# A mixture-of-experts block loop: lists, row split, scaling, gather and transposes in another order

## The chip, the cores and the metric

The kernel runs on one core of a Trainium2 chip. The core has five engines with a queue each: TensorE (PE) multiplies matrices into PSUM, VectorE (DVE) and ScalarE (ACT) work element by element, GpSimd (POOL) does small operations and issues gathers and scatters by index, SyncE (SP) issues the other DMAs. Each engine takes its instructions strictly in program order and waits on semaphores of the others. The metric is the device time of one execution in microseconds; the median of several runs counts.

## What is computed

An attention over pooled keys and values gives rows x of 512 numbers, one a token (8 x 576 = 4608 tokens). Each token is sent to one of 8 experts: a gate picks one, or the token keeps its predecessor's. The part that the change touches is what comes then, for each token:

```python
h = np.maximum(x[b, s] @ w1[e], 0.0)     # 512 -> 1024
out[b, s] = p[e] * (h @ w2[e])           # 1024 -> 512, scaled by the gate's weight
```

Inputs and outputs are float32. The products run on numbers split in two (a high and a low part, the three larger of the four products kept).

## The kernel before

The first 200 us or so are the attention and the routing; they write the rows x to memory (`x_rows`) and the tokens of each expert to lists (`ids`). Then come blocks of 256 listed rows of one expert, in two halves of 128, or of 128 rows alone at the end of an expert's list. Three blocks run in code ahead of the loop; the loop `For_i` runs the others, 14 with two halves and 5 with one in this execution. All instructions of the loop stand in the order in which they are written (`manual_schedule`), for each engine.

Names: `W1` and `W2` are the weights split into high and low tiles (`w1h`, `w1l`, `w2h`, `w2l` in rows), `raw1` and `raw2` the next expert's weights as they arrive (`raw`), `xt` (`x` in rows) the rows split and turned, `ht` the hidden values split (`ht_h`, `ht_l`), `hp` the PSUM tiles of layer 1 (six of them), `o_ps` the two PSUM tiles of layer 2, `ob` the scaled output, `m_a`, `m_b`, `m_c`, `m_d` the lists (token number and weight) of four blocks that follow each other, `idp` a list as it arrives, `idk` row numbers for the gather, `xg` gathered rows, `xd` their copy in memory, `xq` the copy read back in pieces of 32 columns, `xs` the pieces transposed.

A pass of the loop for block j, before the change:

- `entry(iv, 0)` loads from a table whether the block has one or two halves; TensorE, ScalarE and VectorE branch by it.
- `head(j)`: VectorE takes the list that was fetched in the block before (`ids_take`, L295, `row_numbers`, L292); SyncE fetches the list of block j + 3 (`lists`, L289); GpSimd touches `xg` (`seen_x`, L1084), writes into it (`fetch`, L1098 and L1099) and gathers rows (L299).
- Two halves (`two_halves`): eight times eight matmuls of layer 1 (L322, L324), each followed by ScalarE and VectorE (`l1_h`, `l1_l`, L329 to L335), the transposes of `xq` by quarters in between (`squares`, L310), then layer 2 of the second half (`l2(1)`, L346). One half (`l1_one`): 24 matmuls of layer 1 (L976), ReLU (L981), VectorE's transpose of the whole `xq` (L982), eight transposes on TensorE (L985), the split into `ht` (L990, L991).
- `rest(j)`: SyncE writes the gathered rows to `xd` and reads them back in pieces (`rows_pieces`, L303, `pieces_rows`, L307). `changes` loads whether the next block has another expert. If so, `weights1` splits W1 (ScalarE casts, L172, VectorE subtracts, L173) and SyncE fetches further weights (L165). VectorE shifts the lists (`meta_shift`, L1093 to L1095, and L1165), scales the second half's output (`emit_scale(1)`, L1078), and GpSimd scatters it (`emit_rows`, L1087 to L1089). `next_rows` splits the next block's rows (L315, L316). TensorE does layer 2 of the first half (`l2(0)`), `weights2` splits W2 (L177, L178) and SyncE fetches (L169), then follow `emit_scale(0)` and `emit_rows(0)`.

So each queue holds a block's work in this order; a waiting instruction holds up all that stands behind it on its engine. SyncE doesn't wait for TensorE itself and runs ahead into the next block until a gather or a list that isn't taken stops it.

## Time and profile before

| | us |
|---|---|
| median of 3 runs (624.92 to 626.41) | 625.03 |
| profiled execution | 623.03 |
| its span | 621.3 |
| TensorE busy in it | 594.5 |
| VectorE busy | 439.7 |
| ScalarE busy | 291.8 |
| GpSimd busy | 273.6 |

The span is the time from the first instruction to the last; the execution's own time lies around it. Busy times of different engines overlap. A row of a timeline gives the start, the length, the engine, the line in the code, the operation with what it writes and reads, and in brackets how long the engine stood idle before it and what ended that. A matmul's end is modelled, so its length overlaps the next one.

### The profile page before, as it was taken

To read this page: it belongs to the slowest core of one execution; us is meant where nothing else is said; L and a number is where in the kernel's file an instruction comes from. 1 tells how busy PE (TensorE), PEld (TensorE's weight loads), DVE (VectorE), ACT (ScalarE), POOL (GpSimd) and SP (SyncE) were. 2 spreads that over 40 slices of the span, in tenths; PEclk is the share of its full clock that TensorE was granted. 3 is DMA by queue.
4 is the path that set the end of the run, shared out by engine and by line. 5 is a ranking of instruction groups with operands and counts; after the bars stand their busy time and mean duration, and the time that the engine had idled before them with its cause. 6 is when DMAs were issued, how large, how long until landed. Compare 5 with 4: busy or idle time off the path is not lost. (4 is left out here: it accounts for less than half of the span.)

```text
span 621.3 us, 14355 instructions
## 1 busy us (share of the span) xinstructions
PE 594.5 (96%) x3386; PEld 509.3 (82%) x3387; DVE 439.7 (71%) x1035; ACT 291.8 (47%) x697; POOL 273.6 (44%) x505
## 2 busy tenths in 40 slices
PE   8999999999999999999999999999999999999991
PEld 7898988898878878888887877787888888888870
DVE  7899898999766426565885686889556686654781
ACT  2777777965433313242742373746233363422550
POOL 6686776776673425134134326132352213341242
PEclk9999999999999999999999999999999999999996
DMA  8998973975003584331663486577543385322403
GB/s 340 356 383 303 365 276 103 318 173 204 19 2 102 176 301 135 102 118 68 211 228 113 143 259 219 186 242 267 196 127 105 101 258 195 115 71 85 118 27 99
DMA packets 62009, 111.95 MB, mean 180 GB/s; under 512 B 13466, under 2 KB 33946, under 8 KB 61980
## 3 DMA queue, kind: packets, MB, share of 16 engines
q1 hardware_dynamic: 53468, 89.54, 43.5%
q0 software_dynamic: 8512, 22.07, 11.0%
q8 instruction: 13, 0.21, 0.1%
q14 instruction: 16, 0.13, 0.1%
HBM read 81.88 MB, written 31.80 MB: 183 GB/s over the span
## 5 line engine op out<-in xcount | busy, mean ns | idle before, releaser
L322 PE MATMUL hp<-x,w1h 128*128 128x512 f32 x364 | 130.7, 400 | 2.5 <-DVE x L316 2.5
L346 PE MATMUL o_ps<-w2h,ht_h 128*128 128x512 f32 x312 | 122.8, 393 | 1.2 <-ACT ht_h L990 1.2
L346 PE MATMUL o_ps<-w2l,ht_h 128*128 128x512 f32 x312 | 122.1, 391 | 0.4 <-DVE w2l L178 0.2
L324 PE MATMUL hp<-x,w1l 128*128 128x256 f32 x364 | 102.2, 281 | 0.0
L329 ACT COPY hs<-hp 128x256 f32<-128x256 f32 x91 | 33.4, 369 | 125.8 <-PE hp L324 120.5
L346 PE MATMUL o_ps<-w2h,ht_l 128*128 128x512 f32 x312 | 87.8, 391 | 1.4 <-DVE ht_l L991 1.4
L322 PEld LDWEIGHTS hp<-x,w1h 128*128 128x128 f32 x364 | 68.4, 188 | 20.4 <-issue 3.8
L334 ACT ACTIVATE ht_h<-hs 128x256 fp32r<-128x256 f32 x136 | 57.1, 420 | 37.5 <-DVE hs L330 30.4
L1087 POOL TENSOR_TENSOR m_e<-m_i,zi 128x1 int32<-128x1 int32 x42 | 8.5, 201 | 142.3 <-DVE m_i L292 136.4
L346 PEld LDWEIGHTS o_ps<-w2h,ht_h 128*128 128x128 f32 x312 | 58.6, 188 | 14.6 <-issue 2.2
L346 PEld LDWEIGHTS o_ps<-w2h,ht_l 128*128 128x128 f32 x312 | 58.4, 188 | 14.5 <-DVE ht_l L991 2.2
L1078 DVE TENSOR_SCALAR ob<-o_ps,m_a 128x512 f32<-128x512 f32 x42 | 31.5, 750 | 53.9 <-PE o_ps L346 50.6
L324 PEld LDWEIGHTS hp<-x,w1l 128*128 128x128 f32 x364 | 68.9, 189 | 0.7
L346 PEld LDWEIGHTS o_ps<-w2l,ht_h 128*128 128x128 f32 x312 | 58.7, 188 | 12.5 <-DVE w2l L178 1.3
L565 PE MATMUL op<-vaug,aT 128*128 128x148 f32 (+4 forms) x448 | 66.0, 306 | 0.7 <-ACT osb L367 0.6
L565 PEld LDWEIGHTS op<-vaug,aT 128*128 128x128 f32 (+1 forms) x448 | 60.0, 179 | 3.9 <-issue 1.3
L335 DVE SCALAR_TENSOR_TENSOR ht_l<-hs,ht_h 128x256 fp32r<-128x256 f32 x136 | 56.4, 416 | 5.9 <-ACT ht_h L334 5.5
L1088 POOL TENSOR_TENSOR zf<-m_e,ob 128x1 f32<-128x1 f32 x42 | 13.9, 331 | 96.1 <-DVE ob L1078 65.2
L1089 POOL DMA_INDIRECT out<-ob,m_e x42 | 45.8, 1091 | 18.8 <-issue 18.8
L330 DVE TENSOR_TENSOR hs<-hp,hs 128x256 f32<-128x256 f32 x91 | 37.3, 417 | 19.9 <-ACT hs L329 11.5
L704 POOL DMA_INDIRECT ids<-pm,pos x36 | 38.7, 1076 | 17.0 <-DVE pos L699 8.0
L299 POOL DMA_INDIRECT vt_in<-x_rows,idk x40 | 39.8, 995 | 10.1 <-issue 8.1
(256 smaller groups left out, 1170.2 us busy)
## 6 DMA issues: line engine op xcount, KB each, us to landing
raw<-in_moe_w SPq DMA_DIRECT2D x48, 512.0 KB
xd<-vt_in SPq DMA_DIRECT2D x20, 512.0 KB
vt_in<-xd SPq DMA_DIRECT2D x80, 128.0 KB
kk<-in_k SPq DMA_DIRECT2D x16, 576.0 KB
qt<-in_q SPq DMA_DIRECT2D x16, 512.0 KB
vt_in<-in_v SPq DMA_DIRECT2D x16, 512.0 KB
x_rows<-xs SPq DMA_DIRECT2D x16, 512.0 KB
vt_in<-in_v_st SPq DMA_DIRECT2D x8, 256.0 KB
```

What stands on the lines that cost most here:

```text
L299: nc.gpsimd.indirect_dma_start(out=xg[:, h, :], out_offset=None, in_=x_rows[0:NT + 1], in_offset=bass.IndirectOffsetOnAxis(ap=idk[:, h:h + ...
L322: nc.tensor.matmul(out=ps, lhsT=W1[0][:, kk, f * P:(f + 1) * P], rhs=xt[:, kk].rearrange("p i n -> p (i n)"), start=(kk == 0), stop=False, ...
L324: nc.tensor.matmul(out=ps[:, 0:2 * P], lhsT=W1[1][:, kk, f * P:(f + 1) * P], rhs=xt[:, kk, 0, :], start=False, stop=(kk == KD - 1), skip_g ...
L329: nc.scalar.copy(out=hb[:, 0, :], in_=ps[:, 2 * P:])
L330: nc.vector.tensor_tensor(out=hb[:, 1, :], in0=ps[:, 0:2 * P], in1=hb[:, 0, :], op=ALU.add)
L334: nc.scalar.activation(out=ht[0][:, f, :], in_=hb, func=AF.Relu)
L335: nc.vector.scalar_tensor_tensor(out=ht[1][:, f, :], in0=hb, scalar=0.0, in1=ht[0][:, f, :].bitcast(F32), op0=ALU.max, op1=ALU.subtract)
L346: nc.tensor.matmul(out=to[h], lhsT=ht[i][:, kk, h * P:(h + 1) * P], rhs=W2[j][:, kk, :], start=(n == 0), stop=(n == 3 * KF - 1))
L565: nc.tensor.matmul(out=out, lhsT=lhs, rhs=rhs if len(out.shape) == 3 else rhs.rearrange("p s x -> p (s x)"), start=all(x[0] != n for x in ...
L704: ins = nc.gpsimd.indirect_dma_start(out=ids.rearrange("t m w -> (t m) w"), out_offset=bass.IndirectOffsetOnAxis(ap=pos[:, u:u + 1], axis= ...
L1078: nc.vector.tensor_scalar(out=ob[:, h, :], in0=o_ps[h], scalar1=m_a[:, h, 1:2], scalar2=None, op0=ALU.mult)
L1089: return nc.gpsimd.indirect_dma_start(out=outv, out_offset=bass.IndirectOffsetOnAxis(ap=m_e[h][:, 0:1], axis=0), in_=ob[:, h, :], in_offse ...
```

## The change

Nothing is computed otherwise. The list fetched for block j + 3 is taken in block j's `rest`, ahead of the splits of new weights (`take`), and the shift of the lists goes there too; `changes` is loaded at the block's head. SyncE writes `xd` at the head, for rows gathered in the block before. `next_rows` comes ahead of `emit_scale(1)`. Layer 2 of the first half is cut in two: hidden columns 0 to 3 go into the two branches, 4 to 7 stay in `rest`, and behind them GpSimd touches `xg` and gathers (`seen_x`, `fetch`). ScalarE does `emit_scale(0)`. In `l1_one` VectorE's transpose of `xq` comes first, the first four TensorE transposes stand in the middle of layer 1's second half, the other four in the middle of the first part of layer 2, and ReLU runs on 512 columns at once. The block ahead of the loop follows the same `rest`.

```diff
-    def l2(h, kks=range(KF), to=None):
+    def l2(h, kks=range(KF), to=None, part=None):
...
         n = 3 * kks[0]
+        if part:
+            jobs = [jobs[x] for x in part]
+            n += part[0]
...
         def l1_one():
-            for f in range(2):
...
-                for c in range(1 + f):
-                    w = 512 // (1 + f)
-                    nc.scalar.activation(out=hs[:, f * 512 + c * w:f * 512 + (c + 1) * w], in_=hp[f][:, c * w:(c + 1) * w], func=AF.Relu)
-            nc.vector.transpose(out=xs, in_=xq.rearrange("p m (j k) -> p k m j", k=KD))
...
-            turn(0, hp[2])
-            turn(1, hp[5])
...
+            nc.vector.transpose(out=xs, in_=xq.rearrange("p m (j k) -> p k m j", k=KD))
...
+            layer1(0, range(12))
+            relu(0)
+            layer1(1, range(6))
+            turn(0)
+            layer1(1, range(6, 12))
+            relu(1)
+            l2(0, range(4), part=range(6))
+            turn(1)
+            l2(0, range(4), part=range(6, 12))
...
-        def emit_scale(h):
+        def emit_scale(h, late=False):
+            if late:
+                nc.scalar.activation(out=ob[:, h, :], in_=o_ps[h], func=AF.Copy, scale=m_a[:, h, 1:2])
+                return
...
-    def head(j, seen=True):
-        if seen:
-            seen_x(0)
-            seen_x(1)
+    def take():
         ids_take(m_d)
         row_numbers(idk, m_d)
-        lists(j + 3)
-        fetch()
-
-    def rest(j, turned=False):
-        rows_pieces()
+
+    def rest(j, change, begin=False):
+        if begin:
+            rows_pieces()
         pieces_rows()
-        chg, nx = changes(j)
-        first(chg, nx)
         meta_shift()
         nc.vector.tensor_copy(out=m_c, in_=m_d)
-        if turned:
+        take()
+        first(*change)
+        if begin:
             for c2 in range(2):
                 rows_split(c2, hp[3 + c2], xt)
+        else:
+            next_rows()
         seen_o(0)
         emit_scale(1)
         first_half = emit_rows(1)
-        if not turned:
-            next_rows()
-        l2(0)
+        l2(0, range(4, KF))
+        for h in range(2):
+            seen_x(h)
+        fetch()
+        chg, nx = change
         with tc.If(chg > 0):
             weights2(chg, nx)
-        emit_scale(0)
+        emit_scale(0, late=True)
...
             if begin and f == 3:
-                head(1, False)
+                take()
+                lists(4)
+                fetch()
...
         l2(1)
+        if begin:
+            for c2 in range(2):
+                rows_turn(c2, xgs["f"], hp[3 + c2])
+        l2(0, range(4))
...
-            head(iv)
+            change = changes(iv)
+            lists(iv + 3)
+            rows_pieces()
```

On VectorE, in `rest` of a loop block: the shift of the lists, the scaling and the split of the rows, behind W1's splits (rows of REGISTER_ALU and ISA are the queue's own bookkeeping; numbers behind a name tell tiles apart). Before:

```order
L1147 UNCONDITIONAL_BRANCH
L1093 COPY m_a<-m_b 128x4
L292 REGISTER_ALU
L292 CAST m_i<-m_b 128x2
L1095 REGISTER_ALU
L1095 COPY m_b<-m_c 128x4
L1165 REGISTER_ALU
L1165 COPY m_c<-m_d 128x4
L1078 REGISTER_ALU
L1078 TENSOR_SCALAR ob<-o_ps_2348,m_a 128x512
L316 REGISTER_ALU
L316 TENSOR_TENSOR x_2506<-vt_in,x_2506 128x2x256
```

And in the change, from the last shift on:

```order
L1175 COPY m_c<-m_d 128x4
L295 REGISTER_ALU
L295 COPY m_d<-idp 128x4
L292 REGISTER_ALU
L292 CAST idk<-m_d 128x2
L1163 COMPARE_AND_BRANCH
L173 REGISTER_ALU
L173 TENSOR_TENSOR w1l<-raw_2936,w1h 128x1024
...
L316 TENSOR_TENSOR x_2506<-vt_in,x_2506 128x2x256
L1094 ISA
L1094 TENSOR_SCALAR ob<-o_ps_2348,m_a 128x512
```

The shifts and the taking of the list have moved ahead of W1's splits, and the scaling behind the rows' split.

On TensorE, in a block of one half, from layer 1's end to layer 2 (`hs` holds the ReLU, `ident` the identity). Before:

```order
L976 MATMUL hp_2345<-w1h,x_2506 128x512
L985 REGISTER_ALU
L985 MATMUL hp_2346<-ident,hs 128x128 x4
L985 REGISTER_ALU
L985 MATMUL rt<-ident,hs 128x128 x2
...
L1201 UNCONDITIONAL_BRANCH
L346 ISA
L346 MATMUL o_ps_2347<-w2h,ht_h 128x512
```

And in the change:

```order
L987 MATMUL hp_2346<-ident,hs 128x128 x4
L981 MATMUL hp_2345<-w1h,x_2506 128x512
L981 MATMUL hp_2345<-w1l,x_2506 128x512
...
L349 MATMUL o_ps_2347<-w2h,ht_h 128x512
...
L987 MATMUL rt<-ident,hs 128x128 x4
L349 MATMUL o_ps_2347<-w2h,ht_h 128x512
L349 MATMUL o_ps_2347<-w2l,ht_h 128x512
```

The first four transposes now have matmuls of layer 1 behind them, the other four matmuls of layer 2 on both sides.

On GpSimd, over a loop block: the reads and the gather of rows, and the two scatters of the output (`m_e` holds row numbers). Before:

```order
L1084 TENSOR_TENSOR zg<-vt_in 128x1
...
L1098 TENSOR_TENSOR vt_in<-idk,zf 128x2
...
L299 DMA vt_in<-x_rows,idk 128x512 x2
...
L1089 DMA out<-ob,m_e_2332 4608x512
L1087 TENSOR_TENSOR m_e_2331<-m_i,zi 128x1
...
L1089 DMA out<-ob,m_e_2331 4608x512
```

And in the change:

```order
L1105 DMA out<-ob,m_e_2332 4608x512
L1100 TENSOR_TENSOR zg<-vt_in 128x1
...
L1114 TENSOR_TENSOR vt_in<-idk,zf 128x2
...
L299 DMA vt_in<-x_rows,idk 128x512 x2
...
L1103 TENSOR_TENSOR m_e_2331<-m_i,zi 128x1
...
L1105 DMA out<-ob,m_e_2331 4608x512
```

The gather has moved from ahead of both scatters to the place between them.

## Rows read from the trace of the kernel before

**Rows 1.** The page's head: span and instructions.

```profile
span 621.3 us, 14355 instructions
```

**Rows 2.** Waits of TensorE from 225 us on: who waited, for whom, us in total, times, longest.

```profile
PE hp L322 <- DVE x L316: 2.5, 2, 1.3
PE o_ps L346 <- DVE ht_l L991: 1.4, 2, 0.7
PE hp L976 <- DVEq L1197: 0.7, 1, 0.7
```

**Rows 3.** Timeline of TensorE, first one-half block: start, us, operation, idle before.

```profile
234.01 0.39 PE L976 MATMUL hp<-w1h,x 128*128 128x512 f32 x1
234.24 0.60 PE L985 MATMUL hp<-ident,hs 128*128 128x128 f32 x4
234.88 0.71 PE L985 MATMUL rt<-ident,hs 128*128 128x128 f32 x4
235.83 0.47 PE L346 MATMUL o_ps<-w2h,ht_h 128*128 128x512 f32 x1 [0.24 <-ACT ht_h L990]
```

**Rows 4.** The same timeline, a one-half block and the two late block starts.

```profile
374.99 0.96 PE L346 MATMUL o_ps<-w2h,ht_l 128*128 128x512 f32 x3 [0.69 <-DVE ht_l L991]
378.75 0.39 PE L322 MATMUL hp<-x,w1h 128*128 128x512 f32 x1
...
402.25 0.47 PE L322 MATMUL hp<-x,w1h 128*128 128x512 f32 x1 [1.11 <-DVE x L316]
...
425.86 0.47 PE L322 MATMUL hp<-x,w1h 128*128 128x512 f32 x1 [1.35 <-DVE x L316]
```

**Rows 5.** Timeline of VectorE, the block ahead of the first late start.

```profile
395.44 4.63 DVE L173 TENSOR_TENSOR w1l<-raw,w1h 128x1024 fp32r<-128x1024 f32 x4 [2.18 <-ACT w1h L172]
...
400.76 0.75 DVE L1078 TENSOR_SCALAR ob<-o_ps,m_a 128x512 f32<-128x512 f32 x1
401.42 1.28 DVE L316 TENSOR_TENSOR x<-vt_in,x 128x512 fp32r<-128x512 f32 x2
```

**Rows 6.** Timeline of ScalarE: the first one-half block, and the block of rows 5.

```profile
234.44 0.66 ACT L981 ACTIVATE hs<-hp 128x256 f32<-128x256 f32 x2 [1.97 <-PE hp L976]
...
394.16 3.90 ACT L172 CAST w1h<-raw 128x1024 fp32r<-128x1024 f32 x4 [1.36 <-PE o_ps L346]
```

**Rows 7.** ReLU and transposes by line: duration ns min/median/max, first and last start, forms.

```profile
L981 ACT ACTIVATE hs<-hp x15: 378/383/600, 231.9 to 600.2; 128x256 f32<-128x256 f32 x10, 128x512 f32<-128x512 f32 x5
...
L985 PE MATMUL hp<-ident,hs x20: 270/272/273, 234.2 to 600.0; 128*128 128x128 f32 x20
```

**Rows 8.** Waits of SyncE in the whole run: for whom, us in total, times, longest.

```profile
SPq L303 <- DMA vt_in<-x_rows,idk: 80.1, 18, 7.3
SPq L307 <- DMA xd<-vt_in: 47.4, 19, 6.1
```

**Rows 9.** Timeline of SyncE, the one-half block at 365: the copies of a list.

```profile
373.59 2.10 SPq L289 DMA_DIRECT2D idp<-ids  x2
```

**Rows 10.** DMA packets from 376 to 379 us.

```profile
DMA packets 403, 0.53 MB, mean 178 GB/s; under 512 B 273, under 2 KB 273, under 8 KB 403
```

**Rows 11.** The end of the kernel: timelines of TensorE, SyncE and GpSimd.

```profile
606.94 1.07 PE L346 MATMUL o_ps<-w2h,ht_l 128*128 128x512 f32 x4
...
612.63 1.80 SPq L307 DMA_DIRECT2D vt_in<-xd  x4
...
602.02 0.53 POOL L1084 TENSOR_TENSOR zg<-vt_in 128x1 f32<-128x1 f32 x2
...
604.57 0.96 POOL L299 DMA_INDIRECT vt_in<-x_rows,idk  x1 [0.30 <-issue]
...
606.75 0.50 POOL L1088 TENSOR_TENSOR zf<-m_e,ob 128x1 f32<-128x1 f32 x1 [0.84 <-DVE ob L1078]
607.53 1.18 POOL L1089 DMA_INDIRECT out<-ob,m_e  x1 [0.27 <-issue]
...
610.21 1.02 POOL L1089 DMA_INDIRECT out<-ob,m_e  x1 [0.58 <-issue]
```

## The prediction

> **What bounds the kernel now.** I read the page's head first, then whom TensorE waited for in the block loop, then TensorE's timeline at the few places where it waited, and only then the other engines at those places. TensorE is busy nearly all the time, so a gain can only come from its holes, from work that it does without need, and from what lies behind its last matmul. The waits in the loop are few [rows 2]: 2.5 us for x's low half in two waits, 1.4 us for ht's low half in two, 0.7 us at the loop's entry. The shown end of a matmul is modelled, 0.39 us after its start, while the next one starts 0.227 us behind it (four in 1.07 us [rows 11]: (1.07 - 0.39) / 3), so each wait costs 0.16 us more than it shows, and the first matmul after a stop is 0.08 us longer (0.47 us for 0.39 [rows 3]). A further place isn't a wait by the table: in a block of one half 1.82 us go by from the last layer-1 matmul (234.01) to the first of layer 2 (235.83), for eight transposes [rows 3]. The loop has five such blocks (20 transposes of a kind, four a block [rows 7]). The blocks of two halves without new weights run matmul on matmul, and the change can do nothing for them.

> The engine on the path differs by place. Ahead of the two late block starts [rows 4], VectorE splits W1 for 4.63 us, copies the lists, scales the first half of the output (0.75 us), and only then makes x's low half, for whose first part TensorE stands [rows 5]. In the two blocks of one half that follow new weights, VectorE comes late to ht's low half (at 374.99 [rows 4] and once more near 604). Behind the last matmul (606.94 + 1.07 = 608.01) SyncE ends last: it reads row pieces until 612.63 + 1.80 = 614.43 [rows 11], 6.9 us before the span's end.

> **The change part by part.**

> *Transposes among matmuls.* Four transposes take 0.60 us [rows 3], each 0.272 us [rows 7], so they start 0.11 us apart: (0.60 - 0.27) / 3. Set between matmuls, eight cost 0.88 us; with the 0.227 us of the matmul ahead and 0.08 us for one more stop that is 1.19 us, against 1.82 us now: 0.63 us a block. The cover is ScalarE's relu: it starts 0.43 us behind the start of the last matmul that feeds it (234.01 to 234.44), takes 0.60 us for 512 columns instead of 0.38 us for 256 [rows 6, 7], and the transpose follows 0.06 us later (234.44 + 0.38 to 234.88 [rows 3]). That is 1.1 us, and six matmuls stand in between: 7 x 0.227 = 1.6 us. The margin is 0.5 us, less where ScalarE still has a copy of ht ahead. Without that cover each hand-over would show, three a block. The rows show 0.11 us from start to start although one lasts 0.27 us. [...] I go by the spacing.

> *The order on VectorE behind layer 1.* Four small copies now lie between the W1 splits and the scaling (395.44 + 4.63 = 400.07 to 400.76: 0.69 us). They and two more for the list go ahead of the W1 splits, into the 2.18 us in which VectorE waited for ScalarE's first cast; the scaling of 0.75 us goes behind x's split [rows 5]. That makes x's low half 1.44 us earlier. The numbers that tell of new weights are now loaded at the block's head, so a part of ScalarE's 1.36 us ahead of its first cast [rows 6] goes too: bounds 0 and 1.36 us; I take 0.6 us, since the branch stays. Together 2.0 us, against losses of 1.11 + 0.16 = 1.27 us and 1.35 + 0.16 = 1.51 us [rows 4]: both go, with two slow restarts of 0.08 us, **2.9 us**. W2's splits start 1.4 us earlier by the same count, and the last scaling leaves VectorE for ScalarE, so VectorE begins the next block some 2 us earlier. That removes the wait for ht's low half in the last block: 0.69 + 0.16 us and 0.1 us of restart, **0.95 us**; the transpose of the row pieces also goes to that block's start, where its data has long landed.

> *The lists ahead of the splits.* VectorE now takes the next list before the end of the block in which it is fetched, instead of in the block after. Where the list's copies are queued behind new weights, VectorE will stand at them, with x's split behind. In the block at 365 the list copies were issued from 373.59 to 375.69, and 273 small packets still ran between 376 and 379 [rows 9, 10]. With W2's splits 1.4 us earlier, but the row gather moved ahead of the list, I put its landing at 377.2 (bounds 375.7 and 379). Then come two copies, a branch and half of x's split, 1.4 us: the next block starts at 378.6. TensorE's own work there would end at 378.75 - 0.63 - 0.95 = 377.2 [rows 4]. So of this block's 1.6 us next to nothing is left; I count **0**. That leaves four blocks for the first term, 4 x 0.63 = **2.5 us**. The other blocks that follow new weights have two halves and need the list only behind a layer 1 of 64 matmuls instead of 24: free, though the one at 402, where new weights come again at once, is near. In the block before the loop the list is behind the first weights that the loop takes: SyncE's longest wait for row pieces, 6.1 us [rows 8], is at that place, with the list just ahead of them in the queue. VectorE splits x there after the list; I give **-0.3 us** at the loop's entry (bounds 0 and -2).

> *The gather in mid second layer.* Rows are asked for half a block earlier, and SyncE's 80.1 us of waiting for gathers and 47.4 us for the pieces [rows 8] go under matmuls. TensorE waits for none of it in the loop, so it is worth nothing there, except that pieces are no longer late for VectorE. At the end it takes SyncE off the path, but GpSimd now has two gathers between its two scatters: from the release by the first scaling to the scatter's end 2.0 us (606.75 to 608.71), the reads of x and the gathers 3.5 us (602.02 to 605.53), the second scatter with its two small operations 2.5 us (608.71 to 611.23) [rows 11]: 8 us. In the last block VectorE finishes the first scaling about 0.9 us behind the last matmul (ht's low half 2.7 us before it, six copies and a branch 1.6 us, x 1.28 us, scaling 0.75 us). So GpSimd is done 8.9 us after the matmuls, and with 4.4 us for landing and barrier (between 2 us and the 6.9 us of now) the end comes 13.3 us behind them, as now: **0**, bounds -2 and +3.

> *ScalarE scales the last half.* Its 0.60 us for 512 columns from PSUM [rows 7] stand against VectorE's 0.75 us [rows 5]. In the loop six PSUM tiles of layer 1 hide it, at the end the gathers do. Zero.

> Sum: 2.9 + 0.95 + 2.5 - 0.3 = **6.05 us**. The profiled execution took 623.03 us (span 621.3 [rows 1]); the median of three is 625.03, 2 us above it, and I take the difference as fixed: 617.0 us profiled, **619.0 us** as median. By the unknown prices alone 616 to 621.5.

> **The rivals.** *Lists late in more places.* SyncE queues the list behind weights wherever it has just issued them, and the packets after 376 show it [rows 9, 10]. If it costs 1.5 us at 402 and 2 us instead of 0.3 us at the entry, 2.85 us are left: 622.2 us. Against it: the long layer 1 of those blocks. [...]

> *The end shrinks too.* If VectorE scales the first half earlier than I count, SyncE's late pieces become a gain: up to 3 us more, 616 us. For it: SyncE's reads at 612.63; against it: 3.5 us of gathers.

> *VectorE isn't relieved.* If the W1 casts at 394.16 waited for landing weights or for TensorE, which the row names [rows 6], earlier copies bring nothing, 402 and 426 stay, and only the transposes gain: 2.5 - 0.3 = 2.2 us, 622.8 us. Against it: splits, copies, scaling and x follow each other without a hole [rows 5].

> *Slower: TensorE stands inside the blocks of one half.* It now stops in order for ScalarE three times a block, where it stopped once. If hand-overs among running matmuls take 1.1 us longer than the rows say, each stop costs 0.6 us, 5 x 3 x 0.6 = 9 us, 3 us more than all that is won: 628 us. It decides from 0.4 us a stop. Against it: the 0.43 and 0.06 us of the trace.

> **How the numbers follow.** Forecast 0.55; late lists 0.17; shorter end 0.13; VectorE not relieved 0.09; slower 0.06. The range 615.0 to 623.0 takes in the forecast's own, the shorter end and most of the late lists, and leaves out the slower case and the tails of the others. About 0.3% (1.9 us) is what a measurement of this kernel can tell from no change. Faster by more: 0.82 (forecast, end, most of the lists, some of the fourth); within: 0.11; slower: 0.07.

> **What would show it.** Right: layer 1 and layer 2 of a one-half block with only the transposes' 0.88 us between matmuls; no wait for x at the two late starts; none for ht's low half; a wait for x behind the one-half block at 365, with VectorE standing at the list; some 13 us behind the last matmul, with GpSimd last. Wrong: TensorE waiting for ScalarE ahead of transposes, waits for x at starts that had none, or VectorE standing at the list in blocks of two halves.

## The result, and the profile after

The changed kernel takes 633.30 us (median of 4 runs, 632.52 to 634.36) against 625.33 us before (4 runs): a ratio of 1.0126, with an interval of 1.0103 to 1.0149. The forecast was 619 us. It is 8 us slower instead of 6 us faster.

The profiled execution took 632.56 us, before 623.03. Cut at two matmuls that both kernels have (the first of the block ahead of the loop, the last of the kernel), the times are these, in us:

| stretch | before | after | difference |
|---|---|---|---|
| up to the block ahead of the loop | 204.56 | 206.31 | +1.75 |
| from there to the last matmul's start | 403.06 | 401.58 | -1.48 |
| from there to the span's end | 13.67 | 19.94 | +6.27 |
| from the span to the time | 1.74 | 4.73 | +2.99 |

The first line is no effect of the change: the code is the same up to there, and in the thirteen kept traces with that code this stretch takes 201.59 to 208.79 us. The third and the fourth are. All four together put the profiled pair 9.53 us apart, where the medians are 8 us apart. The loop did get shorter, by far less than the sum of its terms. One trace gives its length only roughly: after_pad and after_warm below, which run the same loop, took 400.33 and 398.89 us for it.

The page's head, to [rows 1], and its line for queue 8, whose kind is "instruction" (packets, MB, share of time):

```profile
span 627.8 us, 14379 instructions
...
q8 instruction: 12, 0.20, 0.1%
```

The same line of the kernel before, with one packet more inside the span:

```profile
q8 instruction: 13, 0.21, 0.1%
```

TensorE's waits from 225 us on, to [rows 2] (us in total, times, longest):

```profile
PE hp L981 <- DVEq L1217: 2.4, 1, 2.4
PE hp L322 <- DVE x L316: 2.3, 1, 2.3
```

Of the five waits of before four are gone: the two for ht's low half and the two at the late starts. But the wait at the loop's entry has grown from 0.7 to 2.4 us, and there is one new wait for x's low half. TensorE's timeline shows where (start, us, operation, idle before it):

```profile
338.51 0.60 PE L987 MATMUL hp<-ident,hs 128*128 128x128 f32 x4
338.86 0.48 PE L981 MATMUL hp<-w1h,x 128*128 128x512 f32 x1
...
341.72 0.60 PE L987 MATMUL rt<-ident,hs 128*128 128x128 f32 x4
342.07 0.48 PE L349 MATMUL o_ps<-w2h,ht_h 128*128 128x512 f32 x1
...
232.05 0.47 PE L981 MATMUL hp<-w1h,x 128*128 128x512 f32 x1 [2.35 <-DVEq L1217]
...
382.88 0.47 PE L322 MATMUL hp<-x,w1h 128*128 128x512 f32 x1 [2.31 <-DVE x L316]
```

The first four rows are an undisturbed block of one half, to [rows 3]: four transposes between matmuls cost 0.35 us (338.51 to 338.86), and nothing waits there for ScalarE. The last two are the loop's entry and the start behind the one-half block at 368. VectorE's timeline at both, to [rows 5]:

```profile
228.74 0.17 DVE L295 COPY m_d<-idp 128x4 f32<-128x4 f32 x1 [8.27 <-DMA idp<-ids]
...
229.37 1.29 DVE L285 TENSOR_TENSOR x<-tp,x 128x512 fp32r<-128x512 f32 x2 [0.20 <-DVEq L1163]
...
380.94 0.17 DVE L295 COPY m_d<-idp 128x4 f32<-128x4 f32 x1 [2.50 <-DMA idp<-ids]
381.30 0.17 DVE L292 CAST idk<-m_d 128x2 int32<-128x2 f32 x1 [0.19 <-DVE m_d L295]
382.05 1.29 DVE L316 TENSOR_TENSOR x<-vt_in,x 128x512 fp32r<-128x512 f32 x2 [0.58 <-DVEq L1163]
```

Both times VectorE stands for the list (8.27 us, most of it free, and 2.50 us), and x's split comes right behind the list. What follows the two pauses had no place in the prediction. Busy time by window (us, busy time and count of TensorE, weight loads, VectorE, ScalarE, GpSimd, then TensorE's granted clock, DMA share, GB/s):

```profile
233.50:237.00 3.50, 3.50 (x10) 2.72 (x9) 1.59 (x1) 0.53 (x1) 2.87 (x8) 0.51 0.38 121
239.00:243.00 4.00, 4.00 (x21) 3.32 (x20) 1.31 (x3) 1.49 (x4) 0.37 (x2) 1.00 0.55 200
383.70:387.30 3.60, 3.60 (x14) 3.07 (x13) 0.73 (x2) 0.37 (x1) 2.14 (x7) 0.53 0.54 145
```

The first and the last row lie behind the two pauses. There the granted clock is 0.51 and 0.53, against 1.00 in the row between them, matmuls start 0.43 us apart instead of 0.227, and TensorE loses 1.73 us in the first block (13.59 us instead of 11.86) and 1.56 us in the second (23.79 instead of 22.23).

The end, to [rows 11]: VectorE and GpSimd in the last stretch, the last matmul started at 607.89.

```profile
606.16 0.17 DVE L295 COPY m_d<-idp 128x4 f32<-128x4 f32 x1
608.36 0.17 DVE L292 CAST idk<-m_d 128x2 int32<-128x2 f32 x1 [2.03 <-DMA vt_in<-x_rows,idk]
609.10 1.29 DVE L316 TENSOR_TENSOR x<-vt_in,x 128x512 fp32r<-128x512 f32 x2 [0.57 <-DVEq L1163]
610.31 0.75 DVE L1094 TENSOR_SCALAR ob<-o_ps,m_a 128x512 f32<-128x512 f32 x1
...
611.98 1.02 POOL L1105 DMA_INDIRECT out<-ob,m_e  x1 [0.59 <-POOL zf L1104]
...
614.18 1.00 POOL L299 DMA_INDIRECT vt_in<-x_rows,idk  x1 [0.21 <-issue]
615.49 0.97 POOL L299 DMA_INDIRECT vt_in<-x_rows,idk  x1 [0.31 <-issue]
...
617.51 1.02 POOL L1105 DMA_INDIRECT out<-ob,m_e  x1 [0.57 <-issue]
```

VectorE stands 2.03 us until the gathers that still read the row numbers have landed; only then come x's split and the scaling, and only then the first scatter. The two gathers lie between the two scatters. Then GpSimd drains (one line's instructions: duration ns min/median/max, first and last start):

```profile
L1265 POOLq DRAIN  x5: 40/88/8079, 617.6 to 627.6; - x5
```

The drain of 8.08 us starts at 617.57 while the last scatter still runs and ends at 625.65, 7.12 us behind that scatter's end (618.53); the barrier takes the rest to 627.8.

The same line of the kernel before, and the end of its chain of work (start, us, what), had not been read for the prediction:

```profile
L1243 POOLq DRAIN  x5: 40/88/6936, 611.6 to 621.0; - x5
```

```profile
609.44 0.19 POOL zf L1088
...
610.21 1.02 POOL out L1089
611.23 0.20 issue
611.43 0.07 POOLq L1197
611.50 0.16 POOL ob L1081
```

The chain ended with GpSimd's scatter, not with SyncE, and the drain lasted until 618.55, 7.32 us behind that scatter: from the last scatter's end it was 10.1 us to the span's end before, and it is 9.3 us now.

### The profile page after: what moved, and what is told of

It is laid out like the page before. It is cut to its first block, busy times and chain, and to the rows that moved or that the text cites. A ratio compares the mean times of both kernels' runs of the same rounds, so it can differ in the third digit from the quotient of the medians.

```text
span 627.8 us, 14379 instructions
## 1 busy us (share of the span) xinstructions
PE 594.1 (95%) x3386; PEld 512.1 (82%) x3387; DVE 428.6 (68%) x1017; ACT 306.7 (49%) x712; POOL 292.7 (47%) x511
## 5 line engine op out<-in xcount | busy, mean ns | idle before, releaser
L322 PE MATMUL hp<-x,w1h 128*128 128x512 f32 x364 | 132.1, 403 | 2.4 <-DVE x L316 2.3
L1104 POOL TENSOR_TENSOR zf<-m_e,ob 128x1 f32<-128x1 f32 x42 | 33.7, 803 | 106.2 <-DVEq L1191 57.6
L349 PEld LDWEIGHTS o_ps<-w2h,ht_l 128*128 128x128 f32 x312 | 58.6, 188 | 12.5
L349 PEld LDWEIGHTS o_ps<-w2h,ht_h 128*128 128x128 f32 x312 | 58.6, 188 | 12.4
L1105 POOL DMA_INDIRECT out<-ob,m_e x42 | 43.0, 1024 | 23.0 <-issue 14.5
L299 POOL DMA_INDIRECT vt_in<-x_rows,idk x42 | 41.9, 997 | 10.4 <-issue 8.6
L1092 ACT ACTIVATE ob<-o_ps,m_a 128x512 f32<-128x512 f32 x20 | 13.7, 686 | 65.4 <-PE o_ps L349 59.2
```

Of the source, the lines that this page charges most:

```text
L299: nc.gpsimd.indirect_dma_start(out=xg[:, h, :], out_offset=None, in_=x_rows[0:NT + 1], in_offset=bass.IndirectOffsetOnAxis(ap=idk[:, h:h + ...
L322: nc.tensor.matmul(out=ps, lhsT=W1[0][:, kk, f * P:(f + 1) * P], rhs=xt[:, kk].rearrange("p i n -> p (i n)"), start=(kk == 0), stop=False, ...
L349: nc.tensor.matmul(out=to[h], lhsT=ht[i][:, kk, h * P:(h + 1) * P], rhs=W2[j][:, kk, :], start=(n == 0), stop=(n == 3 * KF - 1))
L1104: nc.gpsimd.tensor_tensor(out=zf2[:, h:h + 1], in0=m_e[h].bitcast(F32), in1=ob[:, h, 0:1], op=ALU.mult)
L1105: return nc.gpsimd.indirect_dma_start(out=outv, out_offset=bass.IndirectOffsetOnAxis(ap=m_e[h][:, 0:1], axis=0), in_=ob[:, h, :], in_offse ...
```

## The experiments

"Loop" is the time from the first matmul of the block ahead of the loop to the last matmul's start, "end" from there to the span's end, both from the profiled execution; "above" is time minus span, over all runs of the kernel. Ratios are to runs of the kernel before that were made beside it. What each kernel changes is said below, in the order in which the questions arose.

| kernel | loop | end | above | ratio, interval |
|---|---|---|---|---|
| before | 403.06 | 13.7 | 1.7 to 1.9 | |
| changed | 401.58 | 19.9 | 4.8 to 5.0 | 1.0126, 1.0103 to 1.0149 |
| turns_only | 401.93 | 13.1 | 1.9 to 5.6 | 1.0004, 0.9968 to 1.0039 |
| take_last | 394.77 | 17.7 | 4.1 to 5.3 | 0.9991, 0.9963 to 1.0019 |
| lists_early | 401.83 | 19.7 | 4.7 to 5.0 | 1.0111, 1.0033 to 1.0188 |
| list_scale | 402.83 | 17.3 | 5.0 | one run |
| take_gather | 394.52 | 14.1 | 4.7 to 5.3 | 0.9942, 0.9909 to 0.9975 |
| scale_first | 395.64 | 13.5 | 4.7 | one run |
| changes_late | 395.71 | 14.8 | 4.7 | one run |
| scale_dve | 395.40 | 15.5 | 4.0 | one run |
| after_pad | 400.33 | 23.7 | 1.7 to 1.9 | 1.0191, 1.0160 to 1.0223 |
| take_gather_pad | 395.05 | 17.4 | 1.7 to 1.8 | 0.9943, 0.9928 to 0.9958 |
| after_warm | 398.89 | 19.7 | 1.7 to 1.9 | 1.0077, 1.0028 to 1.0125 |
| take_gather_warm | 394.58 | 14.1 | 1.7 to 1.9 | 0.9896, 0.9846 to 0.9945 |
| before_long | 403.34 | 13.6 | 1.7 to 1.8 | 1.0091, 1.0061 to 1.0121 |
| branch_copy | 402.13 | 13.1 | 4.2 to 5.3 | 1.0043, 1.0015 to 1.0070 |

Some kernels run the same loop: take_gather, take_gather_pad and take_gather_warm take 394.52 to 395.05 us for it. A difference of half a microsecond between two single traces therefore says little.

### The list's place on VectorE: take_last

```diff
         nc.vector.tensor_copy(out=m_c, in_=m_d)
-        take()
         first(*change)
...
         emit_scale(1)
+        take()
         first_half = emit_rows(1)
```

> The changed kernel with one move: in a block's rest VectorE takes the next list (two small copies) behind the scaling of the first half, no longer ahead of the new weights' splits, x's split and the scaling. Theory A (the list's landing is what holds x's low half): the pause of 2.74 us at the loop's entry and that of 2.70 us behind the one-half block near 368 fall under 0.4 us, the matmuls 0.43 us apart behind both pauses go with them (1.7 and 1.6 us), so from the loop's entry to the last matmul 401.6 us become about 393.3; at the end VectorE no longer stands 2.0 us for the gathers that still read the numbers, so the end comes about 17.9 us behind the last matmul instead of 19.9. Median 633.3 - 8.3 - 2.0 = 623. Rival B (the small copies only showed a wait that x's split would meet next, for row pieces or for ScalarE): pauses stay within 0.5 us of what they are, median 631 to 633. Rival C (the low granted clock comes from the transposes set among matmuls, not from the pauses): pauses go, the 0.43 us spacing stays, median 626.

TensorE's waits from 225 us on:

```profile
PE hp L981 <- ACTq L1217: 0.7, 1, 0.7
```

The stretches behind the loop's entry and behind the one-half block, where the changed kernel had the low clock of 0.51 and 0.53 (columns as above):

```profile
231.00:234.50 3.50, 3.50 (x19) 2.94 (x18) 0.00 (x1) 0.60 (x1) 2.10 (x5) 1.00 0.97 260
378.00:381.60 3.60, 3.60 (x22) 3.09 (x21) 1.18 (x3) 1.49 (x5) 2.80 (x6) 1.00 0.51 167
```

The pause behind the one-half block is gone, the one at the entry is back to what it was before (1.12 us from start to start, not under 0.4 as expected; another engine releases it, and the list has nothing to do with that part), and so is the low clock (1.00 in both rows): the two blocks take 11.95 and 22.23 us. The loop is 394.77 us, 6.8 us shorter than in the changed kernel and 8.3 us shorter than before. The end is 2.3 us shorter. Theory A holds, B and C fall. The three losses hung on one line.

### The list's place in SyncE's queue: lists_early and list_scale

```diff
         take()
+        lists(j + 4)
         first(*change)
...
-            lists(iv + 3)
```

> The changed kernel with the next list's copies issued on SyncE right behind the take, ahead of new weights' loads, instead of at the next block's head behind them; nothing moves on VectorE. If the list is late because it is queued behind weights (theory A), the pause behind the one-half block near 368 goes (2.5 us and 1.6 us of slow matmuls), and the one at the loop's entry stays at 2.5 to 2.9 us with its slow matmuls, since that list is issued ahead of the loop: median about 629.2. If the list is late because SyncE comes late to it or because its many small packets are slow in themselves (rival), the pause near 368 stays over 2 us: 632 to 634.

The entry stayed as expected (2.78 us), the pause near 368 did not go (2.22 us for 2.70). VectorE's timeline there, and GpSimd's ahead of it:

```profile
381.23 0.17 DVE L295 COPY m_d<-idp 128x4 f32<-128x4 f32 x1 [0.19 <-DVE m_c L1175]
383.44 0.17 DVE L292 CAST idk<-m_d 128x2 int32<-128x2 f32 x1 [2.04 <-DMA vt_in<-x_rows,idk]
...
370.88 4.44 POOL L1104 TENSOR_TENSOR zf<-m_e,ob 128x1 f32<-128x1 f32 x1 [7.87 <-DVE ob L1094]
375.47 1.03 POOL L1105 DMA_INDIRECT out<-ob,m_e  x1 [0.15 <-POOL zf L1104]
```

SyncE's issue of that list, in the changed kernel and here:

```profile
369.30 3.75 SPq L169 DMA_DIRECT2D raw<-in_moe_w  x4
376.18 1.96 SPq L289 DMA_DIRECT2D idp<-ids  x2
```

```profile
363.93 1.47 SPq L289 DMA_DIRECT2D idp<-ids  x2
```

Half of theory A holds: issued ahead of the weights, the list isn't waited for (0.19 us where it was 2.50). In the changed kernel the list's 256 packets of 8 bytes run from 378.62 on, right behind the last weight packet of their queue (378.61), here from 365.32 on, ahead of the weights (367.08). But the edit also issued the list 15 us earlier against the block's start, and between issue and first packet lie 2.44 us there and 1.39 us here. So at this block waiting behind weights in the DMA queue makes about 1 us of the delay, and the rest goes with SyncE's issuing the list later. At the loop's entry I take the queue for the cause: the list is issued at 218.43 and its packets run from 226.07 to 228.02, at the end of the weights'. But a second wait of 2.04 us stood right behind the first: the row numbers can't be written anew until the last gather has read them, and that gather is late. It was the same wait as the 2.03 us at the kernel's end.

The next kernel tried one reason for the late gather, the 4.44 us of a one-column multiplication on GpSimd, by moving the scaling ahead of x's split:

```diff
         first(*change)
+        if not begin:
+            seen_o(0)
+            emit_scale(1)
...
-        seen_o(0)
-        emit_scale(1)
+        if begin:
+            seen_o(0)
+            emit_scale(1)
```

> As lists_early, with the scaling of the first half ahead of x's split again as in the kernel before. In lists_early VectorE stood 2.04 us for the last gather to have read its numbers before it could write new ones, behind the one-half block near 370; the gather was late because GpSimd's one-column multiplication ahead of the first half's scatter lasted 4.44 us, all through VectorE's W2 splits. Theory: with the scaling 1.3 us earlier GpSimd does this multiplication ahead of the W2 splits in about 0.2 to 0.5 us, the gathers come 4 us earlier, the wait of 2.04 us goes and with it the pause of 2.2 us near 385 and its slow matmuls; at the entry nothing changes (2.7 us). In exchange x's split is 0.75 us later behind W1 splits: pauses of 0.5 to 0.8 us at the two late starts. At the end too no wait of 2 us for the gathers. Rival (the gather is late for the scatter's own sake or the DMA engines' load): 368's pause stays at 2 us.

A miss. The multiplication began earlier and lasted longer (5.65 us, from 364.98 to 370.63, again to the end of VectorE's splits), the wait for the gathers was 2.24 us, and the pause grew to 3.25 us, since x's split was now behind the scaling as well.

### The gather's place: take_gather and scale_first

```diff
             lists(iv + 3)
-            rows_pieces()
+            for h in range(2):
+                seen_x(h)
+            fetch()
...
         l2(0, range(4, KF))
-        for h in range(2):
-            seen_x(h)
-        fetch()
```

and the row pieces' write back in the rest, on top of take_last.

> As take_last, and the row gather with its two small reads is back at the next block's head, the row pieces' write in the rest, as before the change. Theory of the end: the program ends a fixed time (9.3 us in the changed kernel, 10.0 before: 7.1 to 7.3 us in which GpSimd drains, and the barrier) behind GpSimd's last scatter, and the gathers between the two scatters put that scatter 3.5 us later. So the end comes 3.5 us earlier than in take_last, about 14.4 us behind the last matmul: median about 619.5. If SyncE's late row pieces set the end instead (rival): 1 us or less earlier than take_last. If pieces come late for VectorE inside the loop, the loop is longer than take_last's by more than 0.5 us.

GpSimd at the end (last matmul's start 603.31):

```profile
605.01 1.02 POOL L1105 DMA_INDIRECT out<-ob,m_e  x1 [0.58 <-ACT ob L1092]
...
607.10 1.02 POOL L1105 DMA_INDIRECT out<-ob,m_e  x1 [0.57 <-issue]
```

The end is 14.1 us instead of 17.7, 3.55 us shorter, as expected; the span ends 9.3 us behind the last scatter again (608.12 to 617.43). The gather in the middle of the second layer gave the loop nothing (394.52 to 394.77) and cost the end 3.55 us. With it back the kernel is faster than before, by 0.3 to 0.9%.

```diff
         first(*change)
+        if not begin:
+            seen_o(0)
+            emit_scale(1)
```

with the same two lines left further down for the block ahead of the loop alone, on top of take_gather:

> As take_gather, with the scaling of the first half ahead of x's split, as in the kernel before. If it was this scaling behind x's split that took away the waits for x's low half at the two starts behind new weights: pauses of 0.6 to 0.8 us there (0.34 and 0.23 from start to start in take_gather, so 0.9 to 1.1), the loop 1.2 us longer; at the end the first scaling is 1.25 us earlier, so the end comes 12.5 to 13 us behind the last matmul instead of 14.1. If the earlier copies of the lists had taken them away: the loop as in take_gather within 0.2 us.

Half a miss. No pause at the two starts behind new weights: the first part of x's low half was ready at 396.90 (396.21 and 0.69 us), TensorE went on at 397.38 without a gap. But W1's splits also began earlier in these two blocks, 15.72 and 15.43 us behind the block's start for 16.98 and 16.42 us in take_gather. So the run shows that the waits can be absent with the scaling ahead, not that its place is worth nothing: counted from the first W1 split, x's split began after 5.98 us in the kernel before, 5.20 us here and 4.55 us in take_gather and the changed kernel. The pauses came elsewhere: 0.44 to 0.50 us from start to start behind each one-half block, since there too x's split is behind the scaling. The end is 0.7 us shorter than in take_gather, the loop 1.1 us longer.

### What took the two waits for x away: changes_late and scale_dve

Both on top of take_gather. The first reads the numbers on new weights in the rest again:

```diff
-            change = changes(iv)
...
+        change = change or changes(j)
         first(*change)
```

> As take_gather, with the numbers that tell of new weights read in the rest again instead of at the block's head. If ScalarE's casts of W1 began late for these numbers (1.36 us of idle time ahead of the first one before, 0.75 us after): they begin 0.6 us later again, and x's low half with them, so TensorE waits 0.4 to 0.8 us at the two starts behind new weights near 402 and 424 (0.34 and 0.23 from start to start in take_gather, so 0.6 to 1.0). If the small copies ahead of the splits alone have taken the waits away: starts as in take_gather within 0.2 us.

ScalarE's first cast of W1 in the block ahead of the first late start, here and in take_gather:

```profile
395.29 1.05 ACT L172 CAST w1h<-raw 128x1024 fp32r<-128x1024 f32 x1 [1.38 <-PE o_ps L349]
```

```profile
395.44 1.05 ACT L172 CAST w1h<-raw 128x1024 fp32r<-128x1024 f32 x1 [0.75 <-DVE m_a L1109]
```

The 0.63 us came back as expected, and with them a pause of 1.26 us at 401.95; none at 424. In the same block VectorE also waited longer for row pieces (2.46 us for 1.16), and the first cast came 1.55 us later behind the block's start, so less than half of it is the numbers'. The second:

```diff
-        emit_scale(0, late=True)
+        emit_scale(0)
```

> As take_gather, with the last half scaled by VectorE again instead of ScalarE. If VectorE's relief by 0.75 us is what took away the wait for ht's low half in the one-half blocks behind new weights: waits of 0.3 to 0.7 us come back in the block near 366 and in the last one, so the loop is 0.3 to 1.4 us longer; elsewhere nothing. If not (the earlier W2 splits suffice): loop 394.5 us within 0.2. At the end the second scatter comes 0 to 0.7 us later.

Pauses of 0.59 and 0.71 us from start to start at the two late starts (0.34 and 0.23 in take_gather), and 0.25 us more in the block at 365. The waits for ht's low half that were expected did not come. The loop is 0.9 us longer than in take_gather, 0.35 us longer than in take_gather_pad, which has the same loop and a pause of 0.65 us at the first of the two starts; the end is 1.4 us longer. So ScalarE's scaling was worth 0.35 to 0.9 us in the loop by this one run, where the prediction gave it zero.

### The transposes alone: turns_only

The new form of the one-half block in the kernel before, nothing else.

> The kernel before with the transposes of a one-half block set among matmuls and nothing else. Each of the five one-half blocks 0.73 us shorter, as two undisturbed ones of the changed kernel are (11.86 for 12.59): 3.65 us at most. Where VectorE comes late (the block near 365, the last one) the wait for ht's low half grows by what TensorE has won, so two of the five may give nothing: 2.2 to 3.65 us, median 621.7 to 623.1. Rival (TensorE stands for ScalarE at the hand-overs, or matmuls behind transposes run slower): no gain, 625 or more.

Waits of TensorE from 225 us on:

```profile
PE o_ps L349 <- DVE ht_l L990: 2.9, 2, 1.4
PE hp L322 <- DVE x L316: 2.5, 2, 1.4
PE hp L981 <- DVEq L1212: 0.7, 1, 0.7
PE o_ps L349 <- DVE vt_in L974: 0.6, 1, 0.6
```

The loop is only 1.1 us shorter, and the spans' medians are 622.05 and 623.30 us. The two undisturbed blocks take 12.11 us, 0.48 us less than before and not 0.73: the next block's start then stands 0.48 us from start to start. What TensorE wins where VectorE is late is waited away again: ht's low half costs 2.9 us in its two waits, against 1.4 us before [rows 2], and a third wait is new. No wait for ScalarE shows, so the slower rival's mechanism is absent. The ratio can't tell the gain, since the time above the span lies between 1.9 and 5.6 us from run to run.

### The time above the span

In after_pad and take_gather_pad 60 transposes stand behind the loop, in a branch that is never taken:

```diff
+    with tc.manual_schedule():
+        none = entry(0, 4, (EN.PE,), NB2)
+        with tc.If(none > NB2 - 1):
+            for _ in range(60):
+                nc.tensor.transpose(out=hp[2][:, 0:P], in_=hs[:, 0:P], identity=ident)
```

> The changed kernel with 60 transposes on TensorE behind the loop, in a branch that is never taken: no work is added but the reading of one number on TensorE after its last matmul, and TensorE's code is longer behind the loop. Seen so far: the time lies 1.7 us above the span in every run of the kernel before, 4.8 us in those of the changed one, and queue 8 moves its last 16 KB at 609 us before and 1.35 us behind the last instruction in the changed kernel. Theory (those 16 KB are TensorE's code, and where they are fetched only after the end the program waits for them): with the longer code the last 16 KB are fetched while the end of the kernel runs, the time is 1.7 to 1.9 us above the span, median 630.2. Rival (another engine's code, or the time above the span has another cause): the difference stays at 4.7 to 5.1 us, median 633.

> As take_gather, with the 60 transposes that are never run. By the theory of the code's last 16 KB the time above the span falls from 4.8 to 1.8 us: median 621.8 - 3.0 = 618.8, faster than both kernels. By the rival 621.8.

Half a miss: the 3 us left the stretch above the span, as the theory had it, and came back inside it. The end grew by 3.8 and 3.3 us, and take_gather_pad's ratio is that of take_gather. In after_pad TensorE stands that long at the branch (duration ns, start):

```profile
L1231 PEldq COMPARE_BRANCH  x1: 3801/3801/3801, 623.7 to 623.7; - x1
```

A transfer of 16 KB of queue 8 runs while it stands there (from 624.81 on in the DMA records; the branch stands from 623.66 to 627.46), in take_gather_pad one from 610.66 on (609.65 to 612.98). The page calls queue 8's kind "instruction", and by its counts I take it to carry TensorE's code: with the one behind the span there are 13 transfers in the changed kernel and in take_gather, and 14 in after_pad and take_gather_pad, where only TensorE's code is longer. So I read the 3.3 to 3.8 us as TensorE waiting for code; no row names what the branch stands for. The next two kernels shorten TensorE's code by 12 matmuls, as many as the change had added (in instructions they are more: in the trace of the kernel before the 18 warm-up matmuls have 36 records, and the 120 of layer 1 in the one-half blocks have 120):

```diff
-            for _ in range(3):
-                nc.tensor.matmul(out=wm[:, 0:P], lhsT=ident, rhs=ident, start=True, stop=True)
+            nc.tensor.matmul(out=wm[:, 0:3 * P], lhsT=ident, rhs=ident.unsqueeze(1).broadcast_to([P, 3, P]), start=True, stop=True)
```

> The changed kernel with the warm-up matmuls at the program's start, 18 of 128 columns, written as 6 of 384 columns: the same time on TensorE, and TensorE's code 12 matmuls shorter, as long as it was before (the change writes the first 12 matmuls of the second layer's first half into both branches). Theory: the 3.1 us that lie between the span and the time more than before hang on where the pieces of 16 KB of TensorE's code fall; with the old length the last one is fetched once more as TensorE leaves the loop, some 10 us ahead of the end, and the time is 1.7 to 1.9 us above the span; 3 us less than the changed kernel, a ratio of 1.010 to 1.014 to the kernel before instead of 1.013 to 1.018. Rival: 4.7 us or more above the span, as in the changed kernel.

> As take_gather, with the warm-up matmuls as in after_warm. By the theory of the code's pieces: loop 394.5 us and end 14.1 us as in take_gather, 1.7 to 1.9 us between span and time: 8 us under the kernel before, ratio 0.987. By the rival 0.993 to 0.995, as take_gather.

All 11 runs lie 1.7 to 1.9 us above their span, with loop and end as expected for take_gather_warm; it takes 616.92 us and has the lowest ratio here, though its interval meets that of take_gather. after_warm's interval is too wide to give the 3 us by its ratio alone. Then the reverse, longer code in the kernel before, at the program's start:

```diff
-            for _ in range(3):
-                nc.tensor.matmul(out=wm[:, 0:P], lhsT=ident, rhs=ident, start=True, stop=True)
+            for c0, c1 in ((0, 64), (64, P), (0, 64), (64, P), (0, P)):
+                nc.tensor.matmul(out=wm[:, c0:c1], lhsT=ident, rhs=ident[:, c0:c1], start=True, stop=True)
```

> The kernel before with 12 of its 18 warm-up matmuls at the program's start split into two of 64 columns: as many columns, TensorE's code 12 matmuls longer (1271 rows of code for 1259; the kernel with the transposes alone has 1270, the changed one 1272). Theory (the time above the span hangs on the length of TensorE's code and on nothing else in the change): some or all runs lie 4 to 5.5 us above their span instead of 1.7, loop and end as before; median 0.3 to 0.5% slower. Rival (something else in the change brings the 3 us, and fewer warm-up matmuls took them away by another way): 1.7 to 1.9 us in every run, ratio 1.000.

A miss: 1.7 to 1.8 us in all six runs. Longer code at the program's start isn't it. (Its ratio says something else: the warm-up row reads

```profile
1.93 13.17 PE L754 MATMUL rt<-ident 128*128 128x64 f32 x60 [1.93 <-POOL ident masks.py:199]
```

so the split warm-up took 13.17 us instead of 6.41 and delayed the first real matmul from 8.17 to 14.89 us.) Last, the twelve matmuls copied where the change copies them, in both branches of the loop's body, with nothing reordered:

```diff
         l2(1)
+        l2(0, range(4))
...
                 l1_one()
+                l2(0, range(4))
...
-        l2(0)
+        l2(0, range(4, KF))
```

> The kernel before, in which the first 12 matmuls of the second layer's first half stand in both branches of a block, as in the changed kernel, and nothing runs in another order in any block: TensorE's code is 12 matmuls longer inside the loop's body. Theory (these copies put TensorE's code so that 3 us come to lie behind the span): the time is 4 to 5.5 us above the span in some or all runs, the span as before, median 0.3 to 0.5% slower. Rival (longer code isn't enough, as in before_long, where the longer code stood at the program's start and every run lay 1.7 us above its span): 1.7 to 1.9 us in every run, ratio 1.000.

4.2 to 5.3 us above the span in all 10 runs, with the loop within 1 us of the kernel before and the spans' median 618.7 us against 619.2; 0.43% slower. The copy alone brings the loss. The kernel before moves the last 16 KB of queue 8 at 609.05, just behind its last matmul; branch_copy, turns_only and the changed kernel 1.1 to 1.9 us behind their last instruction (629.15 in the changed one).

That the 3 us are the program waiting for such a 16-KB transfer is an inference: the records of instructions end with the span, and what speaks for it are the two branches that stood for 3.8 and 3.3 us while one ran. What stays open: after_warm has no transfer of queue 8 at its end, but take_gather_warm has a last one behind its end (615.33, with the span's end at 614.12) and yet lies 1.7 to 1.9 us above the span. So a late transfer in the records doesn't say by itself that the time waits for it.

## Why the prediction was wrong, point by point

*Transposes: right, a little small.* Undisturbed one-half blocks take 11.86 us for 12.59: 0.73 us, where 0.63 was worked out. Once VectorE is in time all five do (11.83 to 11.99 us in take_gather, and 11.63 in the last, which is counted to its last matmul's start). The 0.11 us of spacing was the right price, not the duration of 0.27 us. What the prediction left out is that the term needs the terms on VectorE beside it: alone it shortens the loop by 1.1 us (turns_only).

*x's low half at the two late starts: right.* The three blocks from the one at 376.79 on take 22.23 us each in take_last, against 23.50, 23.61 and 22.32 before: 2.74 us for 2.9. Of the reasons given, the new order behind W1's splits shows directly: x's split begins 4.55 us behind the first of them instead of 5.98, which is 1.43 us where 1.44 was worked out. The earlier numbers took 0.6 us from ScalarE's wait ahead of its first cast, as put; what that alone is worth for x is open, since in changes_late the row pieces were late as well. ScalarE's scaling, put at zero, helped too (scale_dve).

*ht's low half in the last block: right.* The last block is 11.63 us for 13.37: 0.73 us of transposes and 1.01 us, where 0.95 was worked out.

*The list in the block at 365: the landing right, what hangs on it not.* The list let VectorE go 12.4 us behind the block's start (380.94 and 368.56); the prediction had 12.0. But from there to the first matmul it was 1.94 us, not 1.4, and the block took 14.32 us instead of 13.4. The term is -0.76 us instead of 0, and the clock took 1.56 us more. The rival of late lists put its cost at the block at 402 instead, which lost nothing.

*The list at the entry: the near bound taken.* The prediction gave -0.3 us with bounds of 0 and -2, although the row it named, SyncE's longest wait of 6.1 us, was at that place [rows 8]. It was -1.63 us, and -1.73 us by the clock. Two rows that show a transfer behind weights should have weighed more than the lack of a row for the wait itself; the rival of late lists had the mechanism and the price at this place, 2 us, with a chance of 0.17.

*The clock: missing.* No row of before shows TensorE slowing behind a wait; its longest pause there was 1.74 us from start to start, and its granted clock from 225 to 608 us was 1.00. So a late list was priced as its wait, and in the profiled execution it cost twice that or more. In take_last and the kernels built on it, where no pause is longer than 1.3 us, the low clock does not appear in the loop; over the whole span their profiled executions have a clock of 0.988 to 0.992, the changed kernel's 0.980.

*The end: the step that failed most.* The prediction held that SyncE ended last and that 4.4 us lie between GpSimd's last scatter and the span's end. No row showed the 4.4 us; they were the middle of the bounds of 2 and 6.9 us. The chain of work of the kernel before ended with that scatter, and 10.1 us lay behind it, 7.3 of them up to the end of GpSimd's drain. With that row the sum would have been: scaling done 0.9 us behind the matmuls, 8 us of GpSimd, 10.1 us, 19.0 us instead of 13.3: an end 5.7 us longer, with everything else unchanged. The chain of 8 us itself was right (7.5 us from 611.06 to 618.53). What comes on top is the wait of 2.03 us for the gathers, which no part of the prediction had: moving the gather behind the take of one block leaves the next block's take waiting for it.

*The time above the span: not thought of.* "I take the difference as fixed" was wrong by 3 us. branch_copy shows it as the price of writing 12 matmuls twice; by what mechanism stays open.

*Slower, but not by the rival that said so.* That rival's 0.07 rested on TensorE standing for ScalarE in the one-half blocks. No such wait shows, and these blocks got shorter wherever VectorE was in time.

Together: 1.63 - 0.3 and 1.73 at the entry, 0.76 and 1.56 at the one-half block, 6.27 at the end, 2.99 above the span and 1.75 in the unchanged part make 16.4 us. Of that 0.8 us came back: the transposes gave 3.0 us in four blocks instead of 2.5, the waits for x and ht 3.75 instead of 3.85, and blocks of two halves 0.4 us that no term had. The profiled time was foreseen at 617.0 and was 632.56.

## What to carry to other kernels

A wait that is taken earlier in an engine's order becomes a wait for all that stands behind it (2.50 us of VectorE at the list ended in 2.31 us of TensorE in the changed kernel): read what is queued between its old and its new place, and put a copy of late data behind the work that others wait for. Read the end of a kernel from its chain of work and from each engine's last instructions, drains included, before anything is moved to it. And when a change copies code into both branches of a loop, compare time minus span, not only the span (branch_copy: 4.2 to 5.3 us for 1.7 to 1.9, with the spans alike).

## What the runs showed of the hardware

*A GpSimd multiplication that ended with VectorE's splits.* The one-column multiplication ahead of the scatter takes 0.19 us where VectorE has gaps (median, and mean in take_last 0.197 us), but 4.44 us while VectorE makes the four W2 splits, and 5.65 us with x's split ahead of them; both times it ends within 0.1 us of VectorE's last split. In the changed kernel it adds up:

```profile
L1104 POOL TENSOR_TENSOR zf<-m_e,ob 128x1 f32<-128x1 f32 x42 | 33.7, 803 | 106.2 <-DVEq L1191 57.6
```

33.7 us for 42 of them, against 13.9 us in the kernel before and 8.3 us in take_last, where the small list copies stand between scaling and splits. I take these copies for the reason; they were not tried apart. The 4.44 us run through four instructions of VectorE in a row, 4.62 us together (370.65 to 375.27 in lists_early); by what mechanism was not shown.

```profile
231.50:235.00 3.50, 3.50 (x18) 2.83 (x17) 0.83 (x1) 0.60 (x1) 2.87 (x7) 1.00 0.41 121
380.70:384.30 3.60, 3.60 (x23) 3.13 (x22) 1.08 (x3) 1.17 (x3) 2.12 (x7) 1.00 0.51 134
```

The length of the pause alone doesn't decide it; what does stays open.

*GpSimd's drain.* In all sixteen kept traces it ended 7.1 to 7.4 us behind the last scatter's end (7.32 us in the kernel before, 7.12 us in the changed one). Whether a last gather instead of a scatter would change that wasn't tried.
